# A linear-attention and MoE kernel on one core: the products of the queries with kv in two column halves

## The chip, the cores and the metric

The kernel runs on one core of a Trainium2 chip. Its time is device time in microseconds, from three runs: 862.56, 862.80 and 863.41 us, median 862.8 us. One further execution was taken by the hardware profiler; all rows of the profile come from that one. The engines are named as the profile names them: PE is TensorE's matmuls and PEld its weight loads, DVE is VectorE, ACT is ScalarE, POOL is GpSimd, SP is SyncE, whose queue issues the DMAs.

## The reference

Eight batches, eight heads, 576 tokens of 64 values for each head. Attention is linear: queries and keys go through the same feature map, kv and the normalizer z are sums over the keys' tokens, and each query is one product with kv and one with z.

```python
def phi(x):
    proj = np.einsum('bhsd,df->bhsf', x, w_phi)              # 64 -> 128
    proj = proj - np.max(np.abs(proj), axis=-1, keepdims=True)
    return np.concatenate([np.exp(proj), np.exp(-proj)], axis=-1)   # 256 features
q_p, k_p = (phi(q), phi(k))
kv = np.einsum('bhsf,bhsd->bhfd', k_p, v)
z = np.sum(k_p, axis=2)
num = np.einsum('bhsf,bhfd->bhsd', q_p, kv)
den = np.einsum('bhsf,bhf->bhs', q_p, z)[..., None] + 1e-06
return (num / den).astype(np.float32)
```

The heads are then put side by side (512 values a token) and go through the second part: `h = relu(x @ w_in)` with 1024 columns, a convolution of three taps along the tokens of each batch, `gate = sigmoid(conv)`, and `(h * gate) @ w_out` with 512 columns. Everything is float32.

## The kernel before

**Tiling of attention.** Two heads lie in the 128 partitions of one loaded tile, and four heads (two pairs `i` and two pairs `pr`) make a `qd`; a batch has two of these. The tokens of a `qd` come in five groups `g`: groups 1 to 4 hold two tiles of 128 tokens (n = 2), group 0 holds one tile with the last 64 tokens of two head pairs (n = 1). So a batch has ten groups for the keys (`k_process`) and ten for the queries (`q_process`).

**A query group** goes through these steps. `load_split` loads it (line 186) and splits it into two parts (line 71 and 74); `project` multiplies with `w_phi` (lines 203 to 209) and subtracts the largest absolute value on DVE (lines 214 and 216); TensorE transposes the result into the PSUM tile `tp` (line 298); ACT takes the exponential twice, with both signs, into `qe` (line 303), which has the 128 features of one sign and head in its partitions and 128 tokens along the free axis. Then comes the line that the change touches, 321: the product of `qe` with kv. The stationary operand is `qe[:, s, i, t, :]`, 128 features by 128 tokens; the moving operand is `kv`, 128 features by 65 columns (64 values of v and the normalizer), or by 130 in group 0, where two head pairs share a tile. Two such products, one for each sign `s`, accumulate into `ps[:, t, i, :]`, with the tokens in the partitions. A group with n = 2 has 8 products, group 0 has 4; all batches together have 8 x (8 x 8 + 2 x 4) = 576. All operands of this line are float32, and the profile shows two matmuls and two weight loads for each product. DVE then adds 1e-6 to column 64 (line 332), takes the reciprocal (333), and multiplies (335), out of the same PSUM tile into `x`.

**Keys.** `k_process` does the same for the keys without the transposes: ACT writes `ke` (line 242), and lines 253 and 258 take the products of `ke` with v into the PSUM tiles `kv`, copied to `kvf` at line 269.

**MoE.** `x_process` turns the `x` tiles with TensorE into chunks of 386 tokens (lines 375 and 378). There are 12 chunks. `h_part` takes 8 x 12 matmuls of 386 columns for a chunk (line 406), `conv_process` the convolution on POOL and DVE (lines 427 and 433) and the gate, `o_part` 4 x 24 matmuls of 384 columns (line 467). That is 192 matmuls a chunk, 2304 in all.

**The order of the work.** `merge` (line 552) writes the order of TensorE's instructions out. Every process is a generator. `yield pe(n, ns)` says that n TensorE instructions were issued and that the last needs ns; `step` (line 524) adds n to `done` of its kind ("a" for attention with the transposes, "m" for MoE) and moves the planner's time `now` on; it counts 112 ns for each instruction (`ISSUE`). `yield until(...)` waits for work of another process, `yield wait(ns)` for a time. Between two yields nothing of another process is put in. Attention goes first when MoE has reached what `paced()` (line 513) allows for the number of attention's instructions so far, else MoE does as soon as it can run; the allowance is interpolated between the points of `PACE`, and past its last point there is no limit:

```python
PACE = ((750, 0), (3300, 1632), (3600, 2016))
```

The framework's scheduler then places the instructions on the engines by the order of emission and by the priorities that `lead()` raises for work of the other engines.

Of the kernel before, what the change touches and what calls it, by code (L numbers as in the profile page):

```python
# [24 lines left out]
VW = D + 1  # L25
# [19 lines left out]
def kernel(  # L45
# [13 lines left out]
    nc = tc.nc  # L59
# [100 lines left out]
    def pe(n, ns):  # L160
        return ("pe", n, ns)

    def wait(ns):
        return ("wait", ns * LAT)

    def until(*keys):
        return ("until", [k for k in keys if k is not None])

    def set_ready(key, ns=0):
        ready[key] = now[0] + ns * LAT  # L170
# [8 lines left out]
    def load_split(src, b, qd, g, kind):  # L179
        c0, n = group_columns(g)  # L180
        if kind == "q" and 2 * b + qd < NQ_F32:
            raw = sb.tile([P, n * P], F32, name=f"{kind}r{b}_{qd}_{g}", tag="th", bufs=3)
            nc.sync.dma_start(out=raw, in_=src[b, qd, :, c0 : c0 + n * P])
            return n, raw, None
        raw = sb.tile([P, n * P], F32, name=f"{kind}r{b}_{qd}_{g}", tag="tr", bufs=3)
        nc.sync.dma_start(out=raw, in_=src[b, qd, :, c0 : c0 + n * P])
        hi = sb.tile([P, n * P], F32R, name=f"{kind}xh{b}_{qd}_{g}", tag="th", bufs=3)
        lo = sb.tile([P, n * P], F32R, name=f"{kind}xl{b}_{qd}_{g}", tag="tl", bufs=3)
        split(raw, hi, lo, nc.gpsimd, nc.gpsimd)
        return n, hi, lo  # L190

    def project(n, hi, lo, b, qd, g, kind):

        if b == 0 and kind == "k":

            ps = pm.tile([P, n * 256], F32, name=f"{kind}p{b}_{qd}_{g}", tag="m")
        else:
            ps = pg.tile([P, n * 256], F32, name=f"{kind}p{b}_{qd}_{g}", tag="g", bufs=4)
        for t in range(n):
            o = ps[:, t * 256 : (t + 1) * 256]  # L200
            his = hi[:, t * P : (t + 1) * P]
            if lo is None:
                nc.tensor.matmul(out=o, lhsT=his, rhs=wbd_f, start=True, stop=True)
                yield pe(2, 432)
                continue
            los = lo[:, t * P : (t + 1) * P]
            nc.tensor.matmul(out=o, lhsT=his, rhs=wbd_hi, start=True, stop=False)  # L207
            nc.tensor.matmul(out=o, lhsT=his, rhs=wbd_lo, start=False, stop=False)  # L208
            nc.tensor.matmul(out=o, lhsT=los, rhs=wbd_hi, start=False, stop=True)  # L209
            yield pe(3, 351)  # L210
        ps3 = ps.rearrange("p (t f) -> p t f", f=F)
        with lead():
            m = sb.tile([P, 2 * n], F32, name=f"{kind}m{b}_{qd}_{g}", tag="m", bufs=4)
            nc.vector.tensor_reduce(out=m, in_=ps3, axis=AX, op=ALU.max, apply_absolute_value=True)
            pr = sb.tile([P, 2 * n, F], F32, name=f"{kind}s{b}_{qd}_{g}", tag=kind + "s", bufs=2)
            nc.vector.tensor_tensor(out=pr, in0=ps3, in1=m.unsqueeze(2).broadcast_to([P, 2 * n, F]), op=ALU.subtract)  # L216
        return pr

    kv = {}
# [58 lines left out]
    def q_process(b, qd, g):  # L278
        j = 10 * b + QORDER.index((qd, g))

        def back(key, k):
            return (key, j - k) if j >= k else None

        yield until(back("qp", 2))
        with lead():
            n, hi, lo = load_split(qT, b, qd, g, "q")
        yield wait(3000)
        yield until(back("tp", 2))
        set_ready(("qp", j))
        pr = yield from project(n, hi, lo, b, qd, g, "q")  # L290
        yield wait(1700)
        yield until(back("num", 2))
        set_ready(("tp", j))

        tp = pg.tile([P, 2, n, P], F32, name=f"tp{b}_{qd}_{g}", tag="g", bufs=4)
        for t in range(n):
            for i in range(2):
                nc.tensor.transpose(out=tp[:, i, t, :], in_=pr[:, 2 * t + i, :], identity=idn)  # L298
                yield pe(1, 60)
        with lead():  # L300
            qe = sb.tile([P, 2, 2, n, P], F32, name=f"qe{b}_{qd}_{g}", tag="qe", bufs=2)
            for s in range(2):
                nc.scalar.activation(out=qe[:, s], in_=tp, func=AF.Exp, scale=1.0 - 2.0 * s)  # L303
        yield wait(2000)
        yield until(back("num", 1), ("kvq", b, qd))

        if g > 0:
            xorder.append((b, g))
            i = len(xorder) - 1 - NX
            yield until(("xc", last_chunk(*xorder[i])) if i >= 0 else None)  # L310
        else:
            yield until(("xc", last_chunk(b - 2, 0)) if b > 1 else None)


        w = 2 * VW if g == 0 else VW
        p0 = 0 if g == 0 else (g - 1) // 2
        ps = pg.tile([P, n, 2, w], F32, name=f"nm{b}_{qd}_{g}", tag="g", bufs=4)
        for t in range(n):
            for i in range(2):
                for s in range(2):  # L320
                    nc.tensor.matmul(out=ps[:, t, i, :], lhsT=qe[:, s, i, t, :],  # L321
                                     rhs=kv[b, qd][i][:, s, p0 * VW : p0 * VW + w],
                                     start=(s == 0), stop=(s == 1))
                    yield pe(2, 220 if g == 0 else 112)
        parts = [(0, 64, 0), (64, 128, VW)] if g == 0 else [(0, P, 0)]
        with lead():
            dn = sb.tile([P, n, 2], F32, name=f"dn{b}_{qd}_{g}", tag="dn", bufs=4)
            rc = sb.tile([P, n, 2], F32, name=f"rc{b}_{qd}_{g}", tag="rc", bufs=4)
            x = sb.tile([P, n, 2, D], F32, name=f"x{b}_{qd}_{g}", tag="x0" if g == 0 else "x", bufs=4 if g == 0 else NX)
            xs[b, qd, g] = x  # L330
            for a, z, c0 in parts:
                nc.vector.tensor_scalar(out=dn[a:z], in0=ps[a:z, :, :, c0 + D], scalar1=1e-6, scalar2=None, op0=ALU.add)
            nc.vector.reciprocal(out=rc, in_=dn)
            for a, z, c0 in parts:
                nc.vector.tensor_tensor(out=x[a:z], in0=ps[a:z, :, :, c0 : c0 + D],
                                        in1=rc[a:z].unsqueeze(3).broadcast_to([z - a, n, 2, D]), op=ALU.mult)
        set_ready(("num", j))
        set_ready(("xs", b, qd, g), 1500)
# [7 lines left out]
    def last_chunk(b, g):  # L346

        t = first_token(b, g) + (64 if g == 0 else 256)
        return b // 2 * 3 + max(c for c in range(3) if HSTART[c] < t)
# [154 lines left out]
    def lead():  # L504

        return tc.high_priority(offset=ahead[0])
# [45 lines left out]
    def merge():  # L552
        nonlocal moe
        while moe is not None or chains or active:
            while chains and sum(1 for p in active if p[2]) < WINDOW:
                b, x, g, kind = chains.pop(0)

                ahead[0] = AHEAD if b > 0 else None
                active.append([now[0], (k_process if kind == "k" else q_process)(b, x, g), True, ahead[0]])
                p = active[-1]  # L560
                if not step(p, "a"):
                    active.remove(p)
            tm = runnable(moe)
            ta = [(runnable(p), j) for j, p in enumerate(active)]
            ta = [(t, j) for t, j in ta if t is not None]
            can_a = [j for t, j in ta if t <= now[0]]
            can_m = tm is not None and tm <= now[0]
            a_first = done["m"] >= paced()
            if can_a and (a_first or not can_m):
                p = active[can_a[0]]  # L570
                ahead[0] = p[3]
                if not step(p, "a"):
                    active.remove(p)
            elif can_m:
                if not step(moe, "m"):
                    moe = None
            else:

                times = [t for t, _ in ta] + ([tm] if tm is not None else [])
                if not times:  # L580
                    raise RuntimeError(f"stuck: {[p[4] for p in active]} {moe}")
                now[0] = min(times)
# [59 lines left out]
```

## Time and profile before

| What | Value |
|---|---|
| Runs | 862.56 to 863.41 us, median 862.8 us |
| Profiled execution, span | 863.1 us (the page gives no time of it outside the span) |
| TensorE matmuls | busy 841.5 us, 5966 of them, and as many weight loads |
| VectorE, ScalarE, GpSimd | busy 546.5, 388.4 and 278.5 us |
| Line 321, products with kv | 1152 matmuls: 1024 of 65 columns, 128 of 130 |
| Lines 253 and 258, products of the keys with v | 1152 matmuls |
| Lines 406 and 467, MoE | 2304 matmuls |
| Mean granted clock of TensorE | 0.982 of full |

How to read its rows: a group's row has the line, the engine, the operation, the program's names with the output first, the form, the count, then busy time in us and the mean of one in ns, and behind the bar the idle time of the engine just before and what ended it. Matmuls overlap one another, so that the sum of their durations isn't the time they take; the distance from one start to the next is. The chain that ended last is followed back from the last instruction, and its rows give a start, a length and the work. A timeline's row gives start, length, engine, line, operation and count, with neighbours of one kind merged. A row of the stages gives a stretch, its length, then for each engine the busy time with the count in brackets, then the granted TensorE clock, the share of the DMA engines and GB/s.

### The profile page before, as it was taken

The page shows a single profiled execution, that of the slowest core. Times are in us where ns is not written, and L with a number is a line of the kernel's source. Part 1 is how long each engine was busy: PE and PEld are TensorE (multiplying, and loading weights), DVE is VectorE, ACT ScalarE, POOL GpSimd, SP SyncE. Part 2 cuts the span into 40 slices and gives each one's busy share as a digit, 9 for nine tenths or more (in the row PEclk, how much of TensorE's full clock was granted, in tenths as well). Part 3 has the DMA queues.
Part 4 walks back from the last instruction along what each step waited for, and adds up shares of the span by engine and source line. Part 5 has one row for each costly group of instructions (what it writes and reads, how often), then busy time and mean ns, then how long its engine had stood idle before and what let it go on. Part 6 is the DMA issues. An engine that isn't in the chain of part 4 may idle for free.

```text
span 863.1 us, 15654 instructions
## 1 busy us (share of the span) xinstructions
PE 841.5 (98%) x5966; PEld 832.0 (96%) x5966; DVE 546.5 (63%) x1110; ACT 388.4 (45%) x678; POOL 278.5 (32%) x434
## 2 busy tenths in 40 slices
PE   7999999999999999999999999999999999999898
PEld 7898989999999999999999999999999999999898
DVE  6788986776665754666666567575557375664541
ACT  5565643744344425435535434444435334433332
POOL 5565863332332330332332232332223132110110
PEclk9788999999999999999999999999999999999899
DMA  6454412112111211111211111111211211000001
GB/s 188 139 148 124 126 56 54 37 41 67 43 37 55 64 37 45 54 37 52 64 40 47 59 41 41 54 46 37 67 44 34 62 35 37 25 2 28 10 28 46
DMA packets 46586, 48.59 MB, mean 56 GB/s; under 512 B 5296, under 2 KB 44464, under 8 KB 46512
## 3 DMA queue, kind: packets, MB, share of 16 engines
q1 hardware_dynamic: 46512, 47.59, 18.9%
q8 instruction: 48, 0.79, 0.4%
q14 instruction: 26, 0.21, 0.1%
HBM read 38.13 MB, written 9.44 MB: 55 GB/s over the span
## 4 chain that ended last, share of the span: by engine, by line
PE 88%; DVE 6%; ACT 2%; issue 1%; DMA 1%; POOL 0%; SPq 0%; ACTq 0%; POOLq 0%
PE hp L406 24%; PE op L467 23%; PE nm L321 13%; PE kv L258 10%; PE tp L298 3%; PE xt L375 2%; PE kp L207 2%; PE kp L208 2%; PE kp L209 2%; PE qp L207 2%; PE qp L209 2%; PE qp L208 2%; PE kv L253 2%; DMA w_r<-in_w_in_dram 1%; DVE c L433 1%
## 5 line engine op out<-in xcount | busy, mean ns | idle before, releaser
L433 DVE SCALAR_TENSOR_TENSOR c<-h,cw,c 128x191 f32<-128x191 f32 (+3 forms) x256 | 136.2, 560 | 88.1 <-POOL c L427 86.4
L321 PEld LDWEIGHTS nm<-kvf,qe 128*128 128x128 f32 x1152 | 164.1, 195 | 5.6 <-ACT qe L303 5.6
L321 PE MATMUL nm<-kvf,qe 128*128 128x65 f32 (+1 forms) x1152 | 160.2, 269 | 4.8 <-ACT qe L303 4.8
L258 PEld LDWEIGHTS kv<-v,ke 128*128 128x128 f32 x1024 | 145.0, 196 | 4.0 <-ACT ke L242 3.8
L258 PE MATMUL kv<-v,ke 128*128 128x65 f32 x1024 | 142.5, 269 | 2.9 <-ACT ke L242 2.9
L406 PE MATMUL hp<-xh,win_hi 128*128 128x386 f32 x384 | 137.8, 363 | 0.2 <-ACT h L412 0.2
L406 PE MATMUL hp<-xl,win_hi 128*128 128x386 f32 x384 | 137.9, 359 | 0.0
L406 PE MATMUL hp<-xh,win_lo 128*128 128x386 f32 x384 | 136.4, 355 | 0.0
L467 PE MATMUL op<-gh,wout_hi 128*128 128x384 f32 x384 | 135.1, 353 | 0.0
L467 PE MATMUL op<-gh,wout_lo 128*128 128x384 f32 x384 | 134.2, 350 | 0.0
L467 PE MATMUL op<-gl,wout_hi 128*128 128x384 f32 x384 | 134.1, 349 | 0.0
L427 POOL TENSOR_SCALAR c<-h,cw 128x384 f32<-128x384 f32 x96 | 57.2, 597 | 228.6 <-ACT h L412 218.1
L242 ACT ACTIVATE ke<-ks 128x512 f32<-128x512 f32 (+1 forms) x160 | 87.9, 584 | 78.5 <-DVE ks L216 58.8
L412 ACT ACTIVATE h<-hp 128x386 f32<-128x386 f32 x96 | 46.9, 493 | 157.9 <-PE hp L406 150.3
L303 ACT ACTIVATE qe<-tp 128x512 f32<-128x512 f32 (+1 forms) x160 | 79.6, 554 | 47.5 <-PE tp L298 47.1
L71 POOL TENSOR_SCALAR qxh<-qr 128x256 fp32r<-128x256 f32 (+1 forms) x70 | 32.3, 462 | 175.8 <-PE kp L208 130.8
L71 POOL TENSOR_SCALAR kxh<-kr 128x256 fp32r<-128x256 f32 (+1 forms) x80 | 39.1, 489 | 115.5 <-PE kp L208 51.6
L406 PEld LDWEIGHTS hp<-xl,win_hi 128*128 128x128 f32 x384 | 72.8, 190 | 0.1
L406 PEld LDWEIGHTS hp<-xh,win_hi 128*128 128x128 f32 x384 | 72.2, 189 | 0.6 <-ACT h L412 0.6
L406 PEld LDWEIGHTS hp<-xh,win_lo 128*128 128x128 f32 x384 | 72.6, 189 | 0.1
L467 PEld LDWEIGHTS op<-gl,wout_hi 128*128 128x128 f32 x384 | 72.4, 189 | 0.2
L467 PEld LDWEIGHTS op<-gh,wout_hi 128*128 128x128 f32 x384 | 72.4, 189 | 0.2
(68 smaller groups left out, 1475.6 us busy)
## 6 DMA issues: line engine op xcount, KB each, us to landing
v<-in_vt_dram SPq DMA_DIRECT2D x80, 130.0 KB, 2.1
kr<-in_kT_dram SPq DMA_DIRECT2D x64, 128.0 KB, 2.1
qr<-in_qT_dram SPq DMA_DIRECT2D x64, 128.0 KB, 2.1
out_dram<-os SPq DMA_DIRECT2D x32, 192.0 KB, 1.9
w_r<-in_w_in_dram SPq DMA_DIRECT2D x8, 512.0 KB, 3.9
w_r<-in_w_out_dram SPq DMA_DIRECT2D x8, 512.0 KB, 3.7
out_dram<-os SPq DMA_DIRECT2D x32, 96.0 KB, 1.7
kr<-in_kT_dram SPq DMA_DIRECT2D x16, 64.0 KB, 1.9
```

Of the source, the lines that this page charges most:

```text
L71: nc.gpsimd.tensor_scalar(out=hi, in0=src, scalar1=1.0, scalar2=0.0, op0=ALU.mult, op1=ALU.add)
L207: nc.tensor.matmul(out=o, lhsT=his, rhs=wbd_hi, start=True, stop=False)
L208: nc.tensor.matmul(out=o, lhsT=his, rhs=wbd_lo, start=False, stop=False)
L242: nc.scalar.activation(out=e[s], in_=pr, func=AF.Exp, scale=1.0 - 2.0 * s)
L258: nc.tensor.matmul(out=kp[i][:, s, p0 : p0 + VW], lhsT=lhsT, rhs=v[:, (2 * t + i) * VW : (2 * t + i + 1) * VW], start=False, stop=(g % 2 = ...
L303: nc.scalar.activation(out=qe[:, s], in_=tp, func=AF.Exp, scale=1.0 - 2.0 * s)
L321: nc.tensor.matmul(out=ps[:, t, i, :], lhsT=qe[:, s, i, t, :], rhs=kv[b, qd][i][:, s, p0 * VW : p0 * VW + w], start=(s == 0), stop=(s == 1))
L406: nc.tensor.matmul(out=ps, lhsT=w_, rhs=x_[:, p, :], start=(k == 0), stop=(k == 11))
L412: nc.scalar.activation(out=hs, in_=ps, func=AF.Relu)
L427: nc.gpsimd.tensor_scalar(out=cv, in0=hs[:, o : o + TC], scalar1=cw[:, f, 1:2], scalar2=0.0, op0=ALU.mult, op1=ALU.add)
L433: nc.vector.scalar_tensor_tensor(out=cv[:, lo:hi], in0=hs[:, o + j - 1 + lo : o + j - 1 + hi], scalar=cw[:, f, j : j + 1], in1=cv[:, lo:hi ...
L467: nc.tensor.matmul(out=ps, lhsT=w_, rhs=x_, start=(i == 0), stop=(i == 23))
```

## The change

Each product of line 321 is taken as two, over the tokens 0 to 63 and 64 to 127 of the tile: the stationary operand has 64 columns instead of 128, and the output is the lower or the upper 64 partitions of the same PSUM tile. Operand kv, its 65 or 130 columns, the accumulation over `s` and the steps behind are as they were. The two halves alternate within the innermost loop. There is one `yield` for the whole group now, which counts 16 n instructions and 100 ns, instead of one for each product with 2 instructions and 112 or 220 ns; so nothing of another process stands between the products of a group in the order of emission, and attention's count in `done` grows by 8 n more for each group.

```diff
         for t in range(n):
             for i in range(2):
                 for s in range(2):
-                    nc.tensor.matmul(out=ps[:, t, i, :], lhsT=qe[:, s, i, t, :],
-                                     rhs=kv[b, qd][i][:, s, p0 * VW : p0 * VW + w],
-                                     start=(s == 0), stop=(s == 1))
-                    yield pe(2, 220 if g == 0 else 112)
+                    for a in (0, 64):
+                        nc.tensor.matmul(out=ps[a : a + 64, t, i, :], lhsT=qe[:, s, i, t, a : a + 64],
+                                         rhs=kv[b, qd][i][:, s, p0 * VW : p0 * VW + w],
+                                         start=(s == 0), stop=(s == 1))
+        yield pe(16 * n, 100)
         parts = [(0, 64, 0), (64, 128, VW)] if g == 0 else [(0, P, 0)]
```

## The prediction

> **What bounds the kernel now.** I read the page's busy times and chain first, then the stages, then TensorE's own rows. From the page of the kernel before:
>
> ```profile
> span 863.1 us, 15654 instructions
> ...
> PE 841.5 (98%) x5966; PEld 832.0 (96%) x5966; DVE 546.5 (63%) x1110; ACT 388.4 (45%) x678; POOL 278.5 (32%) x434
> ...
> PE 88%; DVE 6%; ACT 2%; issue 1%; DMA 1%; POOL 0%; SPq 0%; ACTq 0%; POOLq 0%
> ...
> L321 PEld LDWEIGHTS nm<-kvf,qe 128*128 128x128 f32 x1152 | 164.1, 195 | 5.6 <-ACT qe L303 5.6
> L321 PE MATMUL nm<-kvf,qe 128*128 128x65 f32 (+1 forms) x1152 | 160.2, 269 | 4.8 <-ACT qe L303 4.8
> ```
>
> TensorE is busy from end to end and is 88% of the chain that ended last, so time saved on it is saved from the span wherever no other engine is close behind. The line to be changed, L321, shows 1152 loads and 1152 matmuls: 576 products in the code, each carried out as two passes, each pass with its own load. Busy sums of overlapping matmuls (269 ns of one) are no price; the price is the spacing. From the chain of waits, in order of time:
>
> ```profile
> 63.86 3.63 PE nm L321 x32
> ...
> 474.11 1.73 PE nm L321 x16
> ...
> 759.18 3.52 PE nm L321 x32
> ...
> 826.18 33.38 PE op L467 x192
> ```
>
> The two runs of 32 give (3.63 + 3.52) / 64 = 112 ns a pass, so L321 costs 1152 x 112 = 129 us. A MoE matmul of 384 columns costs 33.38 / 192 = 174 ns. What sets the 112? From the timeline of TensorE, then of its weight loads, first a stretch in which products stand singly between MoE matmuls (three windows of it, the third so late that only the second pass is still in it):
>
> ```profile
> 231.05 0.33 PE L321 MATMUL nm<-kvf,qe 128*128 128x65 f32 x2
> 231.19 0.42 PE L406 MATMUL hp<-xh,win_hi 128*128 128x386 f32 x1
> 231.45 0.22 PE L321 MATMUL nm<-kvf,qe 128*128 128x65 f32 x1
> ...
> 231.11 0.27 PE L321 MATMUL nm<-kvf,qe 128*128 128x65 f32 x1
> ```
>
> ```profile
> 406.70 1.86 PEld L258 LDWEIGHTS kv<-v,ke 128*128 128x128 f32 x16
> ```
>
> Here the second pass started 231.11 - 231.05 = 0.06 us after the first. So the 65 columns themselves need about 56 ns; I use 56. The other half of the 112 is the load: the sixteen loads of L258, the same shape, end 1.86 us after the first began, and with some 190 ns for the last one alone that is 1.67 / 15 = 111 ns from load to load. From 231.05 to 231.45 one product and one MoE matmul took 0.40 us, so the product costs 0.40 - 0.17 = 0.23 us for its two passes, or 113 ns each: the alternation with MoE matmuls gives almost nothing.
>
> Is 111 ns the array's load or the rate at which instructions are handed to it? The end of the kernel answers (timeline, and the row of the stages for that stretch):
>
> ```profile
> 802.09 3.83 PE L321 MATMUL nm<-kvf,qe 128*128 128x130 f32 x16 [3.35 <-ACT qe L303]
> ...
> 801.20:807.80 6.60, 5.71 (x26) 5.71 (x27) 2.84 (x12) 2.28 (x7) 0.00 (x0) 0.50 0.00 0
> ```
>
> At a granted clock of 0.50 sixteen passes last 3.83 us instead of 1.73 us. Both load and 130-column stream run in the array's clock, so this doesn't fully acquit the sequencer, but nothing in the page's chain names TensorE's queue (PEq). I take the load as the limit: 128 columns of weights in 111 ns, 64 in about 55.
>
> The Trainium skill, "TensorE: Matmul & The Clock Gate", section LDWEIGHTS (loading the stationary operand), has a load take its number of columns divided by 1.2 ns, which is 107 ns for 128 and by estimate 53 ns for 64; the measured 111 agrees within 4%, and 64 columns stand in no row of this trace. By its 53 ns the sum below stays what it is.
>
> **The change, part by part.**
>
> *Removed:* 576 products of two passes with 128-column loads, 129 us of TensorE.
>
> *Added:* 1152 products of 64 columns, 2304 passes. Each has a load of about 55 ns and a stream of 56 ns, as rhs keeps its 65 columns. In program order they go: left half pass 1 and 2, right half pass 1 and 2. No row shows two matmuls or two loads in different halves at once, so I bound the price of a former product (224 ns). From below: both halves run on their own, and it costs two streams, 2 x 56 = 112 ns. From above: load and stream of one pass follow one another, 4 x 111 = 444 ns. Between them lies one load at a time, streams hidden, 4 x 56 = 224 ns. I take the lower side, because in full width a load does run beside a stream:
>
> ```profile
> 808.88 0.34 PE L406 MATMUL hp<-xl,win_hi 128*128 128x386 f32 x1
> 808.88 0.19 PEld L406 LDWEIGHTS hp<-xh,win_lo 128*128 128x128 f32 x1
> ```
>
> The load begins as the matmul before it begins; each half would keep a waiting set of weights in the same way. Allowing 3 ns for each of the two starts (an estimate: the rows show both at the same 0.01 us) that is 118 ns, and 576 x 118 = 68 us: 61 us less.
>
> *Not realized early:* the stages from 30 to 120 us and from 120 to 300 us, all instructions, then the first of them for L321's tile alone:
>
> ```profile
> 30.00:120.00 90.00, 83.62 (x605) 80.33 (x605) 80.90 (x148) 51.71 (x98) 63.91 (x68) 0.91 0.42 124
> 120.00:300.00 180.00, 179.74 (x1331) 178.92 (x1330) 120.53 (x251) 85.12 (x150) 59.78 (x101) 1.00 0.17 49
> ...
> 30.00:120.00 90.00, 21.36 (x171) 20.96 (x170) 7.47 (x28) 0.91 0.42 124
> ```
>
> VectorE is busy 80.90 of 90 us there, so the share of that stage, 171 / 1152 x 61 = 9 us, I count as lost (bounds 0 and 9). From 120 us on VectorE has a third of its time free.
>
> *Switching:* the array goes from full width to halves and back once for each of 80 groups, 160 switches, fewer if groups meet. If it must empty first, a switch costs at most the part of a matmul behind its stream. From the view of line 321:
>
> ```profile
> L321 PE MATMUL nm<-kvf,qe x1152: 217/275/587, 28.8 to 805.5; 128*128 128x65 f32 x176, 128*128 128x130 f32 x16
> ```
>
> The shortest record is 217 ns, the stream 56, so 160 ns; 160 x 0.16 = 26 us at most, 0 if nothing empties. I take half, 13 us. Here a rule speaks against the change: the Trainium skill, "TensorEngine Tiling (Array Packing)", section Tiling Modes, Key Properties, says that changing the mode drains TensorE, and also that tiles load and multiply independently. By its drain the term would be the 26 us; no row here has a switch in it.
>
> *The order of emission:* the group now leaves in one piece, with one `yield`, so no MoE matmul stands between its passes; by the 113 against 112 ns above this is worth nothing either way. But it books 1152 more instructions: attention's total goes from 5966 - 2304 = 3662 to 4814, while `PACE` ends at 3600. MoE work is then emitted as soon as it is ready. Before, batch 7's queries (54 passes of projection, 36 transposes, 144 of L321, 28 of L375 and L378: 262) began at 3662 - 262 = 3400, where the pace has 1632 + 100 x 384 / 300 = 1760 MoE matmuls, while 10 x 96 + 9 x 96 = 1824 could have run (`h_part` of ten chunks, `o_part` of nine); these 64, or 64 x 0.174 = 11 us, fill batch 7's waits. Gone, they cost up to 11 us. On the other side the stage from 30 to 120 us has 90 - 83.62 = 6 us without a matmul that earlier MoE work could fill. Between -6 and +11 I take +2.
>
> No DMA, copy or buffer moves. VectorE's reading of `ps` at L332 and L335 still waits for the last product of the group; rows 0 to 127 are filled as before, in the same bank.
>
> *Sum:* 863.1 - 61 + 9 + 13 + 2 = 826 us. The profiled span is 863.1 us, the page has no time outside it, and the median of the runs is 862.8 us; 0.3 us is nothing here. Forecast 826 us. Its own range: no switching cost, no early loss, the pace a gain of 6, gives 796; all of it, 26, 9 and 11, gives 848; both extremes at once are unlikely, so 802 to 845.
>
> **The rivals.**
>
> *Loads take turns.* One load at a time in the whole array, halves or not, at 56 ns: 2304 x 56 = 129 us, exactly what was removed. For it speaks that loads of full width never follow closer than 111 ns, whatever the stream; against it, that nothing shows them sharing one path when they go to different columns. 863 + 13 + 2 = 878 us; without drains and with a gain by the pace 857, with the full bounds 900.
>
> *Load and stream take turns (the slower side).* In halves the next load waits until the stream before it is over: 111 ns for each half-width pass, 2304 x 111 = 256 us. The same price comes out if a load has a fixed length that 64 columns don't shorten, or if passes are handed out no faster than one in 111 ns. 863 + 127 + 13 + 2 = 1005 us. It decides as soon as a half-width pass costs more than 56 ns. Against it stand the two rows of 808.88 us. The Trainium skill, "TensorE: Matmul & The Clock Gate", section The mechanism, speaks for it: loads pass running matmuls where row groups differ, and both halves use all rows; the rows at 808.88 us show a load beside a matmul of the same rows, into waiting weights, so in full width the trace goes against that reading.
>
> *Only neighbours overlap.* The two passes of one half stay in order, and the right half's first pass runs beside the left half's second, but the next product waits for both: three steps instead of four, 3 x 56 = 168 ns, 576 x 168 = 97 us, 32 us less. With 5 us lost early: 863 - 32 + 5 + 13 + 2 = 851 us, 835 to 868.
>
> *It doesn't do what it says* (both halves' instructions run as full-width ones): that is the price of turns again, and goes with the first two.
>
> **How the numbers follow.** Forecast 0.44, loads in turn 0.27, load and stream in turn 0.15, neighbours 0.14. The range reaches from 802 to 893 us: the forecast, the neighbours and the loads in turn but for their end, which leaves out the 1005 us and some 0.03. A measurement of this kernel tells a change of 0.2% (1.7 us) from none. Faster: 0.44 + 0.10 of the neighbours (below 861) = 0.54 less 0.03 for drains above their bound = 0.51. Within: 0.02 of the neighbours and 0.04 of the turns, 0.06. Slower: the rest, 0.43.
>
> **What would show it.** In the changed kernel's profile L321 should have 2304 matmuls and 2304 loads of 64 columns. Right: 32 passes in about 0.95 us of the chain (30 ns each), loads closer than 55 ns, L321 below 8% of the chain. Loads in turn: 32 passes in 1.8 us. Load and stream in turn: 3.5 us. Switching: a longer step at the first pass of a run and at the next full-width matmul, 0.16 us above what stands there now. Pace: TensorE idle between 740 and 800 us by more than the 2 us of now. Wrong altogether would be a shorter span with unchanged spacing at L321, or L321 halved with the span unchanged.

## The result and the profile after

The changed kernel has a median of 858.4 us (15 runs, 853.7 to 863.0), the kernel before 863.4 us (15 runs, 861.4 to 865.0). The ratio is 0.9944, with an interval from 0.9932 to 0.9957: 5 us faster, clear of noise, and far from the 37 us that were forecast. The profiled execution was the fastest of the fifteen: its span is 851.9 us at a granted TensorE clock of 0.992, and the slowest run had 0.976. So rows are compared below by stage and by spacing, and times by the ratios. The ratios are those of fast runs; two of the six runs of one control below, 1394 us at a granted clock of 0.547 and 884 us at 0.969, were slow and are left out of its ratio.

The page of the changed kernel, the lines that answer to those shown of before:

```profile
span 851.9 us, 17963 instructions
...
PE 820.0 (96%) x7118; PEld 780.4 (92%) x7118; DVE 537.3 (63%) x1110; ACT 389.6 (46%) x678; POOL 275.0 (32%) x434
...
PE 83%; DVE 10%; ACT 3%; issue 2%; DMA 1%; POOL 0%; SPq 0%; ACTq 0%; POOLq 0%; DVEq 0%
...
L322 PEld LDWEIGHTS nm<-kvf,qe 128*64 128x64 f32 x2304 | 84.2, 138 | 22.9 <-issue 12.9
L322 PE MATMUL nm<-kvf,qe 128*64 128x65 f32 (+1 forms) x2304 | 101.6, 234 | 3.8 <-ACT qe L303 2.1
```

The products are on line 322 now and run as 2304 passes over 64 columns. TensorE's share of the chain fell, VectorE's rose. A new item stands behind the loads: 12.9 us in which they waited for nothing that the profile shows. The timeline shows where, here around a stretch of 64 passes, a run of half-width passes with full-width work ahead and behind (TensorE, then the loads):

```profile
185.60 0.34 PE L468 MATMUL op<-gh,wout_lo 128*128 128x384 f32 x1
185.87 2.09 PE L322 MATMUL nm<-kvf,qe 128*64 128x65 f32 x64
187.88 0.66 PE L258 MATMUL kv<-v,ke 128*128 128x65 f32 x4
```

```profile
185.86 1.95 PEld L322 LDWEIGHTS nm<-kvf,qe 128*64 128x64 f32 x64 [0.26 <-issue]
187.88 0.52 PEld L258 LDWEIGHTS kv<-v,ke 128*128 128x128 f32 x4
```

From the first pass to the first instruction behind the stretch 187.88 - 185.87 = 2.01 us go by for 64 passes, 31 ns a pass with the leaving. A stretch of 32 passes between MoE matmuls gives the price without the leaving, and that of the edges:

```profile
207.68 0.33 PE L407 MATMUL hp<-xh,win_lo 128*128 128x386 f32 x1
207.94 1.15 PE L322 MATMUL nm<-kvf,qe 128*64 128x65 f32 x32
209.03 0.44 PE L407 MATMUL hp<-xh,win_hi 128*128 128x386 f32 x1
209.31 0.34 PE L407 MATMUL hp<-xl,win_hi 128*128 128x386 f32 x1
```

It took 209.03 - 207.94 = 1.09 us, so 32 passes more cost 2.01 - 1.09 = 0.92 us: 29 ns a pass, 116 ns a product, where full width took 112 ns a pass and 224 ns a product. The two halves load and multiply at once.

This holds for the 512 products of 65 columns. The 64 products of group 0 have 130 columns, and one group 0 shows what they cost, first before, then in the changed kernel:

```profile
287.82 1.06 PE L321 MATMUL nm<-kvf,qe 128*128 128x130 f32 x8
288.72 0.33 PE L258 MATMUL kv<-v,ke 128*128 128x65 f32 x2
```

```profile
193.31 1.11 PE L322 MATMUL nm<-kvf,qe 128*64 128x130 f32 x16
194.36 0.32 PE L258 MATMUL kv<-v,ke 128*128 128x65 f32 x1
```

The four products took 288.72 - 287.82 = 0.90 us before, 112 ns a pass as with 65 columns, and take 194.36 - 193.31 = 1.05 us now. They gained nothing: one pass for each half goes by in the 111 ns that one full-width pass took. So the line became 512 x (224 - 116) = 55 us cheaper, apart from the edges of the stretches.

And the stretch has edges. The MoE matmul ahead of it takes 0.27 us (185.60 to 185.87) until the next start instead of 0.17. The first half-width load begins only as its own matmul does, not beside the MoE matmul; behind the stretch load and matmul of `kv` begin at the same 0.01 us, so that load wasn't brought in ahead either. All edges of the 32 passes above follow from its rows: from 207.68 to 209.31 us stand two MoE matmuls of 0.17 us and 32 passes of 29 ns, and 1.63 - 0.35 - 0.93 = 0.35 us are left over.

The second place where time went is the middle of the kernel. The stage from 120 to 700 us, first of before, then of the changed kernel:

```profile
120.00:700.00 580.00, 579.07 (x4241) 575.93 (x4240) 363.99 (x750) 261.54 (x456) 177.21 (x300) 1.00 0.17 49
```

```profile
120.00:700.00 580.00, 571.53 (x5090) 546.55 (x5089) 358.97 (x761) 262.55 (x454) 171.86 (x301) 1.00 0.17 49
```

TensorE stood still for 0.9 us of it before, and for 8.5 us now, though VectorE and ScalarE have as much time free in it as before. Switching (the edges) and waiting are the two suspects for the 50 us that are missing.

### The profile page after: what moved, and what is told of

It is laid out like the page before. It is cut to its first block, busy times and chain, and to the rows that moved or that the text cites. A ratio compares the mean times of both kernels' runs of the same rounds, so it can differ in the third digit from the quotient of the medians.

```text
span 851.9 us, 17963 instructions
## 1 busy us (share of the span) xinstructions
PE 820.0 (96%) x7118; PEld 780.4 (92%) x7118; DVE 537.3 (63%) x1110; ACT 389.6 (46%) x678; POOL 275.0 (32%) x434
## 4 chain that ended last, share of the span: by engine, by line
PE 83%; DVE 10%; ACT 3%; issue 2%; DMA 1%; POOL 0%; SPq 0%; ACTq 0%; POOLq 0%; DVEq 0%
PE hp L407 23%; PE op L468 23%; PE kv L258 10%; PE nm L322 9%; PE tp L298 3%; PE xt L376 3%; PE kp L207 2%; PE qp L207 2%; PE qp L209 2%; PE qp L208 1%; PE kp L208 1%; PE kp L209 1%; PE kv L253 1%; DVE ks L216 1%; DVE km L214 1%
## 5 line engine op out<-in xcount | busy, mean ns | idle before, releaser
L434 DVE SCALAR_TENSOR_TENSOR c<-h,cw,c 128x384 f32<-128x384 f32 (+3 forms) x256 | 131.3, 545 | 77.7 <-POOL c L428 75.8
L258 PE MATMUL kv<-v,ke 128*128 128x65 f32 x1024 | 131.0, 273 | 5.5 <-ACT ke L242 5.3
L258 PEld LDWEIGHTS kv<-v,ke 128*128 128x128 f32 x1024 | 126.3, 192 | 9.8 <-ACT ke L242 7.9
L407 PE MATMUL hp<-xl,win_hi 128*128 128x386 f32 x384 | 132.3, 345 | 0.0
L407 PE MATMUL hp<-xh,win_lo 128*128 128x386 f32 x384 | 130.5, 340 | 0.0
L468 PE MATMUL op<-gh,wout_hi 128*128 128x384 f32 x384 | 129.7, 339 | 0.0
L322 PEld LDWEIGHTS nm<-kvf,qe 128*64 128x64 f32 x2304 | 84.2, 138 | 22.9 <-issue 12.9
L322 PE MATMUL nm<-kvf,qe 128*64 128x65 f32 (+1 forms) x2304 | 101.6, 234 | 3.8 <-ACT qe L303 2.1
L74 DVE TENSOR_TENSOR gl<-c,gh 128x768 fp32r<-128x768 f32 x48 | 45.1, 964 | 61.3 <-ACT gh L69 61.2
L214 DVE TENSOR_REDUCE km<-kp 128x4 f32<-128x512 f32 (+1 forms) x80 | 50.3, 633 | 35.4 <-PE kp L209 34.6
```

The lines of the kernel that those rows point to most:

```text
L74: eng_lo.tensor_tensor(out=lo, in0=src, in1=hi.bitcast(F32), op=ALU.subtract)
L258: nc.tensor.matmul(out=kp[i][:, s, p0 : p0 + VW], lhsT=lhsT, rhs=v[:, (2 * t + i) * VW : (2 * t + i + 1) * VW], start=False, stop=(g % 2 = ...
L322: nc.tensor.matmul(out=ps[a : a + 64, t, i, :], lhsT=qe[:, s, i, t, a : a + 64], rhs=kv[b, qd][i][:, s, p0 * VW : p0 * VW + w], start=(s = ...
L407: nc.tensor.matmul(out=ps, lhsT=w_, rhs=x_[:, p, :], start=(k == 0), stop=(k == 11))
L434: nc.vector.scalar_tensor_tensor(out=cv[:, lo:hi], in0=hs[:, o + j - 1 + lo : o + j - 1 + hi], scalar=cw[:, f, j : j + 1], in1=cv[:, lo:hi ...
L468: nc.tensor.matmul(out=ps, lhsT=w_, rhs=x_, start=(i == 0), stop=(i == 23))
```

## The experiments

Times below are worked out as ratio times 863.4 us, so that kernels of different calls can be set side by side. The number of stretches is counted in each program's order.

**The order alone.** Full-width products, with the changed kernel's `yield`:

```diff
-                    yield pe(2, 220 if g == 0 else 112)
+        yield pe(16 * n, 100)
```

> Products of 128 tokens as before; only the yields are those of the changed kernel (one for each group, counting 16 n instructions). Theory switching (the gain at the products is given back where the array changes between full width and halves): there is no switch here, so the time stays at that of before, 859 to 867 us. Theory order (it is given back because the counts let MoE's work out too early and TensorE waits later): the order is the changed kernel's, so it is slower than before by what was lost there, 873 to 890 us.

Measured 1.0137 (1.0090 to 1.0184): 12 us slower, 875 us, at the low end of what theory order gave. The order of the changed kernel costs time without any half-width pass. Its stage from 120 to 700 us:

```profile
120.00:700.00 580.00, 572.77 (x4069) 568.66 (x4068) 342.31 (x722) 253.18 (x434) 161.94 (x286) 0.97 0.16 47
```

The 7.2 us of standing still are close to the 8.5 us of the changed kernel. Here the clock also fell to 0.97 in this stage; the runs at a clock of 0.984 to 0.986 took 871 us, those at 0.969 up to 884 us. So 8 us of the 12 are the order at the clock of before, and the rest goes with the lower clock. Between this control and the changed kernel, which has the same yields, lie 17 us; with 55 us saved, 108 stretches cost (55 - 17) / 108 = 0.35 us each.

**Halves in the order of before.** The halves, with a `yield` for each product as before:

```diff
-        yield pe(16 * n, 100)
+                    yield pe(2, 220 if g == 0 else 112)
```

> Halves as in the changed kernel, but the yields of before, one for each product with 2 instructions, so that the order is close to before's and the products stand in some 248 runs between full-width matmuls instead of 108. Theory switching, at 0.26 us for each run: 863 - 55 + 248 x 0.26 = 872 us, slower than before. Theory order: all of the 55 us come through, 808 to 825 us.

Measured 1.0474 (1.0453 to 1.0496): 41 us slower than before. The order is close to before's, the products are 55 us cheaper, and yet the kernel loses. With 248 stretches that makes (41 + 55) / 248 = 0.39 us for each. Its timeline, where products stand singly between MoE matmuls:

```profile
155.24 0.34 PE L322 MATMUL nm<-kvf,qe 128*64 128x65 f32 x4
155.51 0.44 PE L407 MATMUL hp<-xl,win_hi 128*128 128x386 f32 x1
155.88 0.34 PE L322 MATMUL nm<-kvf,qe 128*64 128x65 f32 x4
156.14 0.44 PE L407 MATMUL hp<-xh,win_lo 128*128 128x386 f32 x1
```

One product and one MoE matmul take 155.88 - 155.24 = 0.64 us, against 0.40 us for such a pair before. The four passes would cost 0.12 us and the MoE matmul 0.17, so 0.35 us are the two switches of one stretch. Theory switching holds, at a higher price than the 0.26 us that I had read off the edges.

**The count and the pace.** Two ways to take MoE's early start back: the group counts 8 n as the products did before, or the points of the pace move.

```diff
-        yield pe(16 * n, 100)
+        yield pe(8 * n, 112)
```

> The changed kernel, but the one yield of a group counts 8 n instructions, as many as before, so that the pace and the planner's time go on as before; 96 runs of products. Theory switching alone: like the changed kernel, 852 to 860 us. Theory order alone: 808 to 825 us. Both, with switching at 0.26 us a run: 863 - 55 + 25 = 833 us.

```diff
-PACE = ((750, 0), (3300, 1632), (3600, 2016))
+PACE = ((986, 0), (4338, 1632), (4733, 2016))
```

> The changed kernel with the points of the pace moved by 4814/3662, so that MoE is allowed at the same share of attention's work as before; the planner still books 16 n instructions for a group; 105 runs of products. Theory switching alone: 852 to 860 us. Theory order, by way of the pace: as the kernel that counts 8 n, 808 to 840 us; if that one is faster and this one isn't, it is the planner's time of a group and not the pace.

Measured 0.9800 (0.9777 to 0.9824), 846 us, and 0.9780 (0.9762 to 0.9798), 844 us. Both get 12 to 14 us more than the changed kernel. Since moving the pace alone does it, it is the pace and not the planner's time of a group. The waits in the middle are gone with it, as the stage of the kernel with the moved pace shows:

```profile
120.00:700.00 580.00, 579.63 (x5169) 557.11 (x5168) 368.10 (x767) 267.64 (x463) 181.67 (x305) 1.00 0.17 49
```

0.4 us of standing still. Neither reaches the 808 us of the theory that order alone was to blame.

**The same order without halves**, as a control for the kernel that counts 8 n:

```diff
-                    yield pe(2, 220 if g == 0 else 112)
+        yield pe(8 * n, 112)
```

> Products of 128 tokens in full width, with one yield for a group that counts 8 n instructions: the order of the kernel with halves that counts 8 n (847.5 us), without halves. It shows what putting a group's products in one piece is worth by itself. Theory: nothing, 860 to 868 us. Then the halves in that order bring 864 - 847.5 = 16 us, and with 55 us saved at the products 96 stretches cost 0.40 us each. Rival: the one piece hurts too, as in the first control (880 us); then a stretch costs more, up to 0.55 us.

Measured 1.0062 (1.0042 to 1.0081): 5 us slower than before, 869 us, just above the theory's numbers. So one piece for each group costs a little. Between this control and the halves in that order lie 23 us; with 55 us saved, 96 stretches cost (55 - 23) / 96 = 0.34 us each.

**More switches, nothing else.** In the kernel that counts 8 n two products of each group of two tiles go in full width, amid the others:

```diff
-                    for a in (0, 64):
-                        nc.tensor.matmul(out=ps[a : a + 64, t, i, :], lhsT=qe[:, s, i, t, a : a + 64],
+                    for a, z in [(0, P)] if (n, t, i) == (2, 0, 1) else [(0, 64), (64, P)]:
+                        nc.tensor.matmul(out=ps[a:z, t, i, :], lhsT=qe[:, s, i, t, a:z],
```

> The kernel with halves that counts 8 n, in which two of the eight products of each group of two tiles (tile 0, pair 1) are taken in full width, in the middle of the group, so that 64 groups have one stretch more, 158 instead of 96. The 128 products cost (224 - 117) x 128 = 14 us more by themselves. Theory, 0.38 us a stretch: 847.5 + 14 + 62 x 0.38 = 885 us. Rival (a switch itself costs no more than 0.16 us, the rest is order and waits): 847.5 + 14 + 10 = 871 us; switching free: 861 us.

Measured 1.0166 (1.0141 to 1.0191), 878 us, between the theory's 885 and the rival's 871: 32 us above the kernel that counts 8 n. The program has 154 stretches, not the 158 of the expectation. Less the 14 us of the full-width products themselves, 58 more stretches cost 18 us, 0.30 us each, give or take 0.05 by the two intervals. This price has no change of the pace in it. That it is the lowest of the prices fits the trace: behind these additional stretches stand passes of 65 columns, and the first of those is delayed less than a MoE matmul. Behind the stretch of 64 passes of the changed kernel, in two later windows:

```profile
188.04 0.39 PE L258 MATMUL kv<-v,ke 128*128 128x65 f32 x2
...
188.15 0.39 PE L258 MATMUL kv<-v,ke 128*128 128x65 f32 x2
```

From the first pass to the second 188.04 - 187.88 = 0.16 us go by, then 0.11 us as in full width: 0.05 us more. The MoE matmul of 209.03 us took 0.28 us instead of 0.17: 0.11 us more.

**No alternation.** The loop over the halves outside the others:

```diff
-        for t in range(n):
-            for i in range(2):
-                for s in range(2):
-                    for a in (0, 64):
+        for a in (0, 64):
+            for t in range(n):
+                for i in range(2):
+                    for s in range(2):
```

> The kernel with halves that counts 8 n, with the loop over the halves outside: a group's products go first for tokens 0 to 63, then for tokens 64 to 127; as many instructions, 105 stretches instead of 96. Theory (two halves run side by side only where neighbouring products go to different halves): a pass costs a whole stream again, 32 passes of a group take 1.8 us instead of 0.96 us, and the time is 847.5 + 55 + 3 = 905 us. Rival (half-width loads alone make a product cheap): 32 passes stay near 1 us and the time near 850 us.

Measured 1.0419 (1.0402 to 1.0437), 53 us above the kernel that counts 8 n. Its chain of waits has, among many alike:

```profile
323.87 1.83 PE nm L322 x32
```

1.83 / 32 = 57 ns a pass: a whole stream each, although each load has only 64 columns. That it is the stream and not the load of 64 columns (by estimate 111 / 2 = 55 ns, nearly as long) shows at the passes of 130 columns: in this trace their starts lie most often 110 ns apart, with loads of the same size. The gain hangs on neighbours in different halves and not on the smaller loads.

**More work in halves.** The keys' products with v (lines 253 and 258) in halves too, in one piece for each group, on top of the kernel that counts 8 n:

```diff
-                    lhsT = e[s][:, 2 * t + i, :]
+                    for a in (0, 64):
+                        lhsT = e[s][:, 2 * t + i, a : a + 64]
...
-                        nc.tensor.matmul(out=kp[i][:, s, p0 : p0 + VW], lhsT=lhsT,
+                            nc.tensor.matmul(out=kp[i][a : a + 64, s, p0 : p0 + VW], lhsT=lhsT,
...
-                        yield pe(2, 112)
+        yield pe(8 * n, 112)
```

> The kernel that counts 8 n, and the keys' products with v (lines 253 and 258) in halves too, one yield for each group that counts 8 n; 165 stretches in halves instead of 96. Theory, 0.38 us a stretch: 847.5 - 55 + 69 x 0.38 = 819 us. Rival (VectorE and ScalarE take over as the limit once TensorE has this much less to do): 835 us or more, with TensorE waiting for them from 120 us on.

and with groups held back until two can go together (the lines of the planner that decide it):

```diff
...
+            held = [j for t, j in ta if t <= now[0] and id(active[j]) in half]
+            go = held and (last[0] or len(held) > 1 or now[0] - half[id(active[held[0]])] > HOLD)
...
```

> The same with both kinds of products in halves, but the planner holds a group's products back, 6 us of its time at most, until a second group is ready, and puts both out together: 138 stretches instead of 165. Theory, 0.38 us a stretch: 10 us less than the kernel with both in halves, 809 us if that one has 819. Rival (holding a group back costs more in waits than the stretches bring): the same time or more.

Measured 0.9595 (0.9573 to 0.9617), 828 us, and 0.9528 (0.9504 to 0.9552), 823 us: both beat both kernels. The first falls 9 us short of its number, and the second 14 us. The stage from 30 to 120 us says why, first of the kernel that counts 8 n, then of the one with both products in halves:

```profile
30.00:120.00 90.00, 81.49 (x781) 74.62 (x780) 83.93 (x152) 52.66 (x100) 67.02 (x71) 0.90 0.41 124
```

```profile
30.00:120.00 90.00, 72.42 (x953) 61.67 (x954) 83.23 (x149) 52.24 (x101) 65.28 (x68) 0.94 0.39 120
...
400.00:700.00 300.00, 300.00 (x3188) 279.84 (x3183) 195.06 (x396) 136.86 (x239) 92.85 (x158) 1.00 0.17 49
```

TensorE stands still 9 us longer there while VectorE stays at 83 to 84 of 90 us: early on VectorE is as close a limit as TensorE. What the rival says of VectorE fits this stage, but not the time from 120 us on that it named: TensorE is busy 300.00 us of the 300 between 400 and 700 us. Pairing saved 6 us for 27 stretches, 0.2 us each. The rest of their price may have gone back in waits: TensorE was busy 67.97 of the 90 us from 30 to 120 us, against 72.42 without pairing.

## Why the prediction was right or wrong

- *The price of a product* was right for the 512 products of 65 columns: 118 ns forecast, 116 ns measured within a stretch. The prediction gave the other 64 the same stream of 56 ns, though its own row of line 321 has the form of 130 columns; those took 112 ns a pass in full width and gained nothing. That is the difference between the 61 us forecast and the 55 us saved. That the halves run side by side, the step with no row behind it, is shown by the 29 ns a pass and by the 57 ns without alternation. Loads in turn, load and stream in turn and neighbours alone are all refuted for this line: 32 passes would have taken 1.8, 3.5 or 1.35 us, and took 1.09 us. (That full-width loads never follow closer than 111 ns was read too strictly: 49 of the 5965 steps in the trace of before are of 30 to 102 ns. No term rests on it.)
- *The switching* is the term that failed, by its size. I took 13 us, half of a bound of 26 us, which was 160 switches times the tail of one matmul, 0.16 us. A stretch, which is two switches, costs 0.30 us where it was measured by itself, 0.34, 0.35 and 0.39 us in three other pairs of kernels, and 0.35 us by the rows of one stretch. So the bound of 2 x 0.16 us for a stretch was close to the whole price, and taking half of it had no reason behind it. And there are 108 stretches for 80 groups, as some groups are split. 108 x 0.30 to 0.39 is 32 to 42 us. Whether the array empties, or the loads that aren't brought in ahead on the way in and out make the price, the rows don't separate.
- *The order of emission* failed too: +2 us taken, -6 to +11 as bounds, 12 us measured by the control with full-width products. The cause that I named is right (the count of `done` runs ahead of `PACE`); the place was wrong. I looked for the waits in batch 7, from 740 to 800 us, where TensorE stood still for 3.3 us instead of 2.1; most came between 120 and 700 us, 8.5 us instead of 0.9, where the chain of the changed kernel has MoE's matmuls in whole blocks:

```profile
229.37 8.35 PE op L468 x48
```

  These are all 48 matmuls of two output tiles with nothing between them. That MoE's work is then missing as filler for attention fits this, and moving the pace took 14 us back. Between the two full-width controls the same change of the count is worth 6 us, part of it clock; why it costs more with halves wasn't tried.
- *Alternation with MoE matmuls*, costed at nothing by 113 against 112 ns, was worth at most the 5 us by which the control that counts 8 n is slower than before; these are part of the 12 us above.
- *The share not realized early* (9 us) wasn't measured for this change alone: TensorE's time without work from 30 to 120 us grew from 6.4 to 10.2 us, which has switching and order in it too. That VectorE limits this stage is shown by the kernel with both products in halves.
- *The sum* in the experiments' terms: 863.4 - 55 + 108 x 0.30 to 0.39 + 12 = 853 to 863 us, around the 858.4 us measured. The direction held, and the gain was given back at the edges of the stretches and to the pace. That 858 us lies within the stated range of 802 to 893 us is luck: the forecast's own range ended at 845 us, and the rivals that stretched it, neighbours alone (835 to 868 us) and loads in turn, are refuted.

What stays open: what the edges consist of inside TensorE; whether the 0.39 us of lone products, against 0.35 us by the rows, is order and waits; and why the control with the changed order fell to a lower clock in some of its runs. No run left the products of group 0 in full width, where by the rows above halves cost a stretch and bring nothing.

## What to carry to other kernels

Narrow products in column halves pay when many of them stand together: here a stretch costs about 0.3 us and a product saves 0.1 us, so three or four products must go in one piece before anything is gained, and the two halves must alternate instruction by instruction. They pay only where a full-width pass takes longer than its stream: with 65 columns (a stream of 56 ns in a pass of 112) the price of a product halved, with 130 columns nothing was gained. Price every form of a line by itself. A mode that costs something at its edges is costed by the number of edges in the program's real order, not by the number of calls in the source. Where an order is paced by a count of instructions, changing how many instructions a step has changes the pace; rescale it with the same edit, or a gain on the bound engine turns into waits.

## What the runs showed of the hardware

Half-width loads into the two halves run at once: 64 passes with 64 loads in 2.01 us, where sixteen full-width loads came 111 ns apart. Within one half passes follow one another at the time of their stream, 57 ns with 65 columns and most often 110 ns with 130, with loads of 64 columns in both. Going into halves and back cost 0.35 us between MoE matmuls: lone products took 0.64 us with their MoE matmul instead of 0.40 us, 0.24 us more for a product whose passes are 0.1 us shorter.
